# Chunked attention on one core: each half of a group's inverse T finished for itself, the second in the group's own first slot

## The chip, the cores and the metric

The kernel runs on one core of a Trainium2 chip. The core's engines are named as the profile names them: PE (matmuls) with its weight loads PEld, DVE (vector work), ACT (activations and copies), POOL (more vector work), SP (issues most DMAs). PSUM is the memory that PE writes into, SBUF the one that all engines share. The time is device microseconds of one execution, and the median of several executions is what is compared.

## What is computed

Three stages follow each other: a recurrent attention over 4 batches, 8 heads, 768 steps and 40 dimensions per head; a mixture of 8 experts of which each token takes one; and a second two-layer network.

```python
for t in range(S):                       # attention, state is D x D for each batch and head
    y[:, :, t] = r_t @ state
    Sa = state @ a_t
    state = state * w_t - outer(Sa, b_t) + outer(v_t, k_t)
...
expert_idx = argmax(x @ w_gate)          # experts: one of 8 for each token
out[mask] = gate_w * (relu(x[mask] @ w1[e]) @ w2[e])
...
h = x @ w_in                             # second network
return (max(h, 0) + alpha * min(h, 0)) @ w_out
```

## The kernel before

**Groups and slots.** The recurrence is cut into chunks of 64 steps. Four chunks (256 steps) of two batches form a group, so there are six groups: three one after the other for each pair of batches. A group is worked off in eight slots, one for each chunk and batch, 48 slots in all. A slot n runs `stage_a` (`sa`, L650) of its own, then `stage_v`, `stage_p` (`pp`, L610, with its copy `pw`, L612) and `stage_r` (`rp`, L638) of slot n + 1, then its `stage_c` (`yc`, L666) and later `stage_d`. All six groups' slots are one chain through the state `sm`.

**What a group needs before its first slot.** `prepare` makes scans of the decay on DVE (`s`, L455, and `q`, L457) and multiplies on POOL (`kb`, L460, and `abd`, L464; on DVE for `kb` in the start group). `products` multiplies them on PE for each of four sets `pg` and two chunks: `lp` (L483), whose parts ACT copies to `l1` and `l2` (L484, L485) and DVE masks into `la` (L491); `sides` adds two transpositions on PE, `bp` (L503) and `ap` (L507). Each of these three takes a bank of the PSUM ring `w1`, which has two.

**The inverse T.** From `l1` and `l2` the generator `inverse` makes the triangular inverse T of the group, the tile `tt`, in two halves of two chunks each. It transposes `l2` to `ul` (L522), does 31 steps of a multiplication `tmp` (L539) and a subtraction `ut` (L541) on DVE, has ACT check the result and `l1` (L424, a sum of squares, written to `ul` as waste), transposes `ut` twice on DVE (`ttc`, L547, and `t11`, L548), and copies the diagonal blocks of both halves into `tt` (L553, four instructions for each half, on POOL; on DVE for half 0 of the start group). Then, for each half, `zp` on PE (L567), its copy `z` by ACT (L570), `yp` on PE (L575) and its negated copy into `tt` by ACT (L577). `stage_p` of the first four slots reads half 0, that of the last four half 1. The banks for `zp` and `yp` are from `w1` in the start group, where eight matmuls with ones fill each of them first (`fill`, L238), and from the ring `mg` elsewhere, which has one bank, and from which the 31 steps of every group after the first take their `tmp` as well.

**What sets the order.** The generator stops at each `yield`, and a table places its pieces: with `n0` the first slot of the group before, the first 16 pieces are placed in slot `n0`, the next 4 in slot `n0 + 2`, the rest in slot `n0 + 8`, which is the group's own first. That is the order of the text only. A scheduler then walks over a modelled time line and takes on each engine what it holds ready, earlier text first, so an instruction may stand far from where the text puts it; only the very start, ahead of the first products, has its order written by hand. After the attention the experts and the second network follow; they start when the attention's tokens are there.

Of the kernel before, what the change touches and what calls it, by code (L numbers as in the profile page):

```python
# [19 lines left out]
P = 128  # L20
# [211 lines left out]
def whole(gen):  # L232
    for _ in gen:
        pass
# [49 lines left out]
class Attention:  # L284
# [230 lines left out]
    def inverse(self, o):  # L515

        nc = self.nc
        l1, l2 = o.l1, o.l2
        o.tt = [self.ringed("tt", self.tt) for _ in range(2)]
        ut = self.ut0 if o.start else self.unit()  # L520
        ul = self.pa.tile([P, 32, 32], F32, name="ul", tag="t4", bufs=3)
        nc.vector.transpose(ul, l2.rearrange("p c u j -> p j (c u)"))  # L522
        yield
        for j in range(31):
# [16 lines left out]
            nc.vector.tensor_tensor(ut[:, j + 1:, :m], ut[:, j + 1:, :m], tv, op=ALU.subtract)  # L541
            if j % 2:
                yield
        self.check(ut, ul, 0.01)
        self.check(l1.rearrange("p c u j -> p (c u) j"), ul, 0.01)
        t11, ttc = self.t4("t11"), self.t4("ttc")
        nc.vector.transpose(ttc.rearrange("p c u t -> p t (c u)"), ut)  # L547
        nc.vector.transpose(t11.rearrange("p c u s -> p s (c u)"), ut.rearrange("p t s -> p s t"))  # L548
        for half in range(2):
            for q in (1, 3, 0, 2):  # L550
                r = slice(32 * q, 32 * q + 32)
                eng = nc.vector if o.start and half == 0 else nc.gpsimd
                eng.tensor_scalar(o.tt[half][r, :, :, 32 * q:32 * q + 32], ttc[r, 2 * half:2 * half + 2], 1.0, 0.0, op0=ALU.mult, op1=ALU.add)  # L553
        yield

        lows = [slice(q * 64, q * 64 + 32) for q in range(2)]
# [1 line left out]
        both = [(c2, u, q) for c2 in range(2) for u in range(8) for q in range(2)]  # L558
        for half in range(2):
            if half:  # L560
                yield
            tt = o.tt[half]
            zp = self.work("zp", [P, 2, 8, 32], "w1" if o.start else "mg")
            if o.start:
                self.fill(zp, 8)
            for c2, u, q in both:
                nc.tensor.matmul(zp[lows[q], c2, u], lhsT=l1[highs[q], 2 * half + c2, u, :], rhs=tt[highs[q], c2, u, highs[q]], start=True, stop=True)  # L567
            z = self.pa.tile([P, 2, 8, 32], F32, name="z1", tag="z1", bufs=1)
            for lo in lows:
                nc.scalar.copy(z[lo], zp[lo])  # L570
            yp = self.work("yp", [P, 2, 8, 32], "w1" if o.start else "mg")
            if o.start:
                self.fill(yp, 8)
            for c2, u, q in both:
                nc.tensor.matmul(yp[lows[q], c2, u], lhsT=t11[lows[q], 2 * half + c2, u, :], rhs=z[lows[q], c2, u, :], start=True, stop=True)  # L575
            for lo, hi in zip(lows, highs):
                nc.scalar.activation(tt[lo, :, :, hi], yp[lo], AF.Copy, scale=-1.0)  # L577
            yield
# [119 lines left out]
    def run(self, rt, sp, moe, ctx):  # L698
        tc, nc = self.tc, self.nc
        os = []  # L700
        for bp in range(B // 2):
            for g in range(S // SL):
                o = K()
# [6 lines left out]
        def at(slot, place, fn):  # L710
            plan.setdefault((slot, place), []).append(fn)
# [19 lines left out]
        def start_inverse(o, n0):  # L731
            inv = self.inverse(o)
            at(n0, 0, lambda: [next(inv) for _ in range(16)])
            at(n0 + 2, 1, lambda: [next(inv) for _ in range(4)])
            at(n0 + 8, 0, lambda: whole(inv))

        def first(o):
# [8 lines left out]
        o = os[0]  # L746
# [10 lines left out]
        inv = self.inverse(o)  # L757
# [7 lines left out]
            whole(self.rest())  # L765
        for _ in range(17):
            next(inv)
        self.slots_room()
        at(1, 1, lambda: whole(inv))
        with tc.issue_after(o.last_v.ins), tc.issue_after(o.last_s.ins), tc.issue_after(o.last_g.ins):  # L770
            first(os[1])
        at(2, 0, self.empty)
        start_inverse(os[1], 0)
        for i in range(2, len(os)):
            lay(os[i], per * (i - 1))
# [558 lines left out]
```

## Time and profile before

| | us |
|---|---|
| median of 3 executions | 1142.77 |
| lowest and highest | 1138.71 and 1146.21 |
| the profiled execution | 1138.26 |
| span of its instructions | 1136.5 |
| its slots of group 0, 1, 2, 3, 4, 5 begin at | 86.2, 171.4, 257.6, 327.2, 402.6, 459.1 |
| attention ends at about | 510 |
| last step L541 of the inverse for group 1, 2, 3, 4, 5 ends at | 155.2, 236.6, 298.4, 381.0, 442.2 |

All starts are counted from the start of the span. The time of an execution lies 1.8 us above the span of its instructions. A group is called after its place, 0 to 5, and group 0 is also the start group, since its preparation has no slots to run beside. A boundary is the time between the last step of a group's inverse and the first `sa` of that group.

### The profile page before, as it was taken

How to read it: one execution, taken by the hardware profiler on the slowest of the kernel's cores; microseconds unless marked ns; L12 is line 12 of the kernel's file. 1: busy time of each engine (PE TensorE's matmuls, PEld its weight loads, DVE VectorE, ACT ScalarE, POOL GpSimd, SP SyncE). 2: the span in 40 equal slices, each digit the busy share in tenths (PEclk: the TensorE clock that was granted, in tenths of full speed). 3: DMA queues.
4: the chain of work that ended last, by engine and by line, in shares of the span. 5: the costliest groups of instructions: out<-in, count | busy, mean ns of one | idle time of the engine just before them, and what ended most of it. 6: DMA issues, size and time to landing. Idle time of an engine off the chain costs nothing.

```text
span 1136.5 us, 24811 instructions
## 1 busy us (share of the span) xinstructions
PE 1005.8 (88%) x9597; PEld 888.8 (78%) x9597; DVE 700.4 (62%) x1469; ACT 571.9 (50%) x1441; POOL 546.4 (48%) x496
## 2 busy tenths in 40 slices
PE   2639898879899898798888889999999999999997
PEld 2538777767687687678787769999999999999996
DVE  9865878978859678444699983324444444453542
ACT  3647687767788778774554444432222222121211
POOL 6717476672865624133664445452535343434332
PEclk8659899978899999799899999999999999999999
DMA  4623232322332124325787776430000000000000
GB/s 119 188 68 98 65 81 79 93 74 65 78 101 80 43 46 109 95 66 180 212 276 242 253 234 172 122 110 21 25 24 24 24 25 24 24 24 23 25 1 26
DMA packets 98080, 103.35 MB, mean 91 GB/s; under 512 B 58404, under 2 KB 78884, under 8 KB 97956
## 3 DMA queue, kind: packets, MB, share of 16 engines
q1 hardware_dynamic: 95652, 93.83, 28.8%
q0 software_dynamic: 2304, 7.87, 2.2%
q8 instruction: 78, 1.28, 0.5%
q14 instruction: 46, 0.38, 0.1%
HBM read 79.39 MB, written 22.28 MB: 89 GB/s over the span
## 4 chain that ended last, share of the span: by engine, by line
PE 56%; DVE 19%; ACT 9%; issue 5%; DMA 5%; POOL 4%; SPq 1%; DVEq 0%; ACTq 0%; POOLq 0%
PE ph L238 20%; PE po L238 19%; PE sa L650 2%; PE pp L610 2%; PE lp L483 2%; DMA raw<-in_moe_w_dram 2%; DVE ut L541 2%; DVE tmp L539 2%; PE yc L666 2%; DVE s L455 2%; DVE dec L215 2%; DVE q L457 2%; PE rp L638 1%; DVE dec L216 1%; POOL tt L553 1%
## 5 line engine op out<-in xcount | busy, mean ns | idle before, releaser
L229 POOL TENSOR_TENSOR gl<-g,gh 128x512 fp32r<-128x512 f32 x96 | 123.9, 1294 | 211.1 <-ACT gh L228 132.9
L228 ACT ACTIVATE gh<-g 128x512 fp32r<-128x512 f32 x96 | 60.7, 632 | 249.4 <-DVE g L1224 178.1
L1223 DVE TENSOR_SCALAR g<-ph,al 128x512 f32<-128x512 f32 x96 | 72.1, 751 | 156.9 <-POOL gl L229 79.1
L238 PE MATMUL ph<-x2thi,win 128*128 128x512 f32 x480 | 157.0, 392 | 0.0
L238 PE MATMUL po<-wout,gh 128*128 128x320 f32 x768 | 139.1, 309 | 0.0
L238 PEld LDWEIGHTS po<-wout,gh 128*128 128x128 f32 x768 | 122.0, 188 | 5.4
L238 PE MATMUL ph<-x2tlo,win 128*128 128x512 f32 x288 | 113.5, 394 | 0.0
L238 PE MATMUL po<-we,hh 128*128 128x320 f32 (+1 forms) x480 | 91.8, 317 | 18.5 <-DVE hh L1099 13.7
L238 PE MATMUL ph<-xthi,we 128*128 128x448 f32 (+2 forms) x360 | 96.6, 340 | 3.0 <-DVE hl L1099 2.9
L238 PEld LDWEIGHTS ph<-x2thi,win 128*128 128x128 f32 x480 | 88.5, 188 | 13.2
L238 PEld LDWEIGHTS po<-we,hh 128*128 128x128 f32 (+1 forms) x480 | 74.3, 183 | 24.9 <-DVE hh L1099 16.3
L238 PE MATMUL po<-wout,gl 128*128 128x320 f32 x384 | 82.9, 311 | 0.0
L624 POOL TENSOR_SCALAR_AFFINE_SELECT va<-vg 64x512 f32<-64x512 f32 x48 | 35.3, 734 | 88.3 <-ACT vg L623 59.5
L238 PE MATMUL ph<-xtlo,we 128*128 128x448 f32 (+2 forms) x216 | 73.4, 341 | 0.3 <-DVE xtlo L271 0.3
L464 POOL TENSOR_TENSOR abd<-ra,q 40x512 f32<-40x512 f32 x44 | 62.0, 1409 | 22.2 <-DVE q L457 7.2
L483 PE MATMUL lp<-kb,abd 128*128 128x128 f32 x352 | 56.0, 304 | 17.1 <-DMA tt<-in_kbP_dram 11.0
L238 PEld LDWEIGHTS ph<-xthi,we 128*128 128x128 f32 x360 | 65.5, 192 | 6.9 <-issue 2.5
L1224 DVE SCALAR_TENSOR_TENSOR g<-ph,g 128x512 f32<-128x512 f32 x96 | 66.3, 691 | 3.1
L238 PEld LDWEIGHTS po<-wout,gl 128*128 128x128 f32 x384 | 64.1, 188 | 2.8
L541 DVE TENSOR_TENSOR ut<-ut,tmp 128x31 f32<-128x31 f32 (+15 forms) x186 | 62.7, 337 | 4.1
L610 PE MATMUL pp<-tt,la 128*104 128x128 f32 x384 | 61.2, 307 | 3.9 <-DVE lg L912 2.2
L483 PEld LDWEIGHTS lp<-kb,abd 128*128 128x128 f32 x352 | 47.9, 209 | 19.8 <-POOL abd L464 13.3
(214 smaller groups left out, 2330.2 us busy)
## 6 DMA issues: line engine op xcount, KB each, us to landing
raw<-in_moe_w_dram SPq DMA_DIRECT2D x16, 512.0 KB
rv<-in_rvP_dram SPq DMA_DIRECT2D x48, 160.0 KB
raw<-in_moe_w_dram SPq DMA_DIRECT2D x16, 480.0 KB
kb<-in_kbP_dram SPq DMA_DIRECT2D x44, 160.0 KB
r<-in_moe_w_in_dram SPq DMA_DIRECT2D x10, 512.0 KB
r<-in_moe_w_out_dram SPq DMA_DIRECT2D x10, 512.0 KB
xs_d<-tt SPq DMA_DIRECT2D x8, 560.0 KB
raw<-in_moe_w_dram SPq DMA_DIRECT2D x16, 256.0 KB
```

Source lines behind the costliest of these rows:

```text
L215: nc.vector.scalar_tensor_tensor(t, up, 0xC0000000, t, op0=ALU.bitwise_and, op1=ALU.bitwise_or)
L228: nc.scalar.activation(hi, src, AF.Copy)
L229: return lo_eng.tensor_tensor(lo, src, f32(hi), op=ALU.subtract)
L238: return nc.tensor.matmul(out, lhsT=lhsT, rhs=rhs, start=start, stop=stop)
L455: nc.vector.tensor_tensor_scan(s[:, ::-1], wz[:, 1:][:, ::-1], self.d1s[:, ::-1], 0.0, ALU.mult, ALU.max)
L464: nc.gpsimd.tensor_tensor(abd[r, :, q * C:(q + 1) * C], ra[r], qc[r, :, :C], op=ALU.mult)
L483: nc.tensor.matmul(lp[:, i], lhsT=abd[:, i, c2, :], rhs=kb[:, i, c2, :], start=True, stop=True)
L541: nc.vector.tensor_tensor(ut[:, j + 1:, :m], ut[:, j + 1:, :m], tv, op=ALU.subtract)
L610: nc.tensor.matmul(pp[:, i], lhsT=o.la[x.half][:, x.c2, u, :], rhs=o.tt[x.half][:, x.c2, u, :], start=True, stop=True)
L624: nc.gpsimd.affine_select(x.va[:C].rearrange("p a b c -> p (a b) c")[:, :, D:], x.vg[:C].rearrange("p a b c -> p (a b) c")[:, :, D:], patt ...
L1223: nc.vector.tensor_scalar(g, ph, 0.0, al[:, f:f + 1], op0=ALU.min, op1=ALU.mult)
L1224: nc.vector.scalar_tensor_tensor(g, ph, 0.0, g, op0=ALU.max, op1=ALU.add)
```

## The change

The half of T that the first four slots read is finished alone, and the other half is left for the group's own first slot: the table places two pieces instead of four in slot `n0 + 2`, and diagonal, checks, `zp` and `yp` of half 1 come from slot `n0 + 8`. In the start group half 1 is placed in slot 0 instead of 1. Each of the two transpositions of `ut` becomes two of half the size, `ttc` first, with the diagonal of half 0 between `ttc` and `t11`. The checks come behind them, the first in place on `ut`, the second written to `ttc` as waste, so behind the diagonal of half 1, which reads `ttc`. And `zp` and `yp` take their banks from `mg` for half 0 and for the whole start group, from `w1` for half 1 of the other groups.

```diff
--- before.py
+++ after.py
@@ -541,16 +541,20 @@
             nc.vector.tensor_tensor(ut[:, j + 1:, :m], ut[:, j + 1:, :m], tv, op=ALU.subtract)
             if j % 2:
                 yield
-        self.check(ut, ul, 0.01)
-        self.check(l1.rearrange("p c u j -> p (c u) j"), ul, 0.01)
-        t11, ttc = self.t4("t11"), self.t4("ttc")
-        nc.vector.transpose(ttc.rearrange("p c u t -> p t (c u)"), ut)
-        nc.vector.transpose(t11.rearrange("p c u s -> p s (c u)"), ut.rearrange("p t s -> p s t"))
-        for half in range(2):
+
+        def diagonal(half):
             for q in (1, 3, 0, 2):
                 r = slice(32 * q, 32 * q + 32)
                 eng = nc.vector if o.start and half == 0 else nc.gpsimd
                 eng.tensor_scalar(o.tt[half][r, :, :, 32 * q:32 * q + 32], ttc[r, 2 * half:2 * half + 2], 1.0, 0.0, op0=ALU.mult, op1=ALU.add)
+
+        ttc = self.t4("ttc")
+        for t in range(0, 32, 16):
+            nc.vector.transpose(ttc.rearrange("p c u t -> p t (c u)")[:, t:t + 16], ut[:, t:t + 16])
+        diagonal(0)
+        t11 = self.t4("t11")
+        for t in range(0, 32, 16):
+            nc.vector.transpose(t11.rearrange("p c u s -> p s (c u)")[:, t:t + 16], ut.rearrange("p t s -> p s t")[:, t:t + 16])
         yield
 
         lows = [slice(q * 64, q * 64 + 32) for q in range(2)]
@@ -558,9 +562,12 @@
         both = [(c2, u, q) for c2 in range(2) for u in range(8) for q in range(2)]
         for half in range(2):
             if half:
+                diagonal(1)
+                self.check(ut, ut, 0.01)
+                self.check(l1.rearrange("p c u j -> p (c u) j"), ttc.rearrange("p c u t -> p (c u) t"), 0.01)
                 yield
             tt = o.tt[half]
-            zp = self.work("zp", [P, 2, 8, 32], "w1" if o.start else "mg")
+            zp = self.work("zp", [P, 2, 8, 32], "mg" if o.start or half == 0 else "w1")
             if o.start:
                 self.fill(zp, 8)
             for c2, u, q in both:
@@ -568,7 +575,7 @@
             z = self.pa.tile([P, 2, 8, 32], F32, name="z1", tag="z1", bufs=1)
             for lo in lows:
                 nc.scalar.copy(z[lo], zp[lo])
-            yp = self.work("yp", [P, 2, 8, 32], "w1" if o.start else "mg")
+            yp = self.work("yp", [P, 2, 8, 32], "mg" if o.start or half == 0 else "w1")
             if o.start:
                 self.fill(yp, 8)
             for c2, u, q in both:
@@ -731,7 +738,7 @@
         def start_inverse(o, n0):
             inv = self.inverse(o)
             at(n0, 0, lambda: [next(inv) for _ in range(16)])
-            at(n0 + 2, 1, lambda: [next(inv) for _ in range(4)])
+            at(n0 + 2, 1, lambda: [next(inv) for _ in range(2)])
             at(n0 + 8, 0, lambda: whole(inv))
 
         def first(o):
@@ -765,8 +772,9 @@
             whole(self.rest())
         for _ in range(17):
             next(inv)
+        next(inv)
         self.slots_room()
-        at(1, 1, lambda: whole(inv))
+        at(0, 0, lambda: whole(inv))
         with tc.issue_after(o.last_v.ins), tc.issue_after(o.last_s.ins), tc.issue_after(o.last_g.ins):
             first(os[1])
         at(2, 0, self.empty)
```

What stood on a line of `inverse` stands lower now: diagonal L549, `ttc` L553, `t11` L557, `zp` L574, `z` L577, `yp` L582, its copy L584, `pp` L617, `pw` L619, `sa` L657.

The scheduler's order on PE around `zp` of the start group, before. The number behind a name is the buffer's; `lp_673` is the first product of group 1, and the sixteen fills of `zp` and `yp` stand ahead of this piece.

```order
L567 MATMUL zp_544<-tt0_124,l1_180 32x32 x32
L575 MATMUL yp_588<-z1_585,t11_532 32x32 x32
L483 MATMUL lp_673<-kb0_107,abd0_109 128x128 x4
L503 MATMUL bp_681<-ident_60,kb0_107 128x104 x4
L610 MATMUL pp_904<-tt0_124,la_182 104x128 x4
L621 MATMUL rvp_910<-rv0_399 64x64 x8
L507 MATMUL ap_687<-ident_60,abd0_109 128x104 x4
```

The same place after the change; `lp_755` and `lp_796` are the fourth and the fifth of group 1's eight products.

```order
L483 MATMUL lp_755<-kb1_108,abd1_110 128x128 x4
L503 MATMUL bp_765<-ident_60,kb1_108 128x104 x4
L507 MATMUL ap_771<-ident_60,abd1_110 128x104 x4
L483 MATMUL lp_796<-kb0_107,abd0_109 128x128 x4
L503 MATMUL bp_804<-ident_60,kb0_107 128x104 x4
L507 MATMUL ap_810<-ident_60,abd0_109 128x104 x4
L483 MATMUL lp_817<-kb0_107,abd0_109 128x128 x4
L503 MATMUL bp_825<-ident_60,kb0_107 128x104 x4
L574 MATMUL zp_540<-tt0_124,l1_180 32x32 x32
```

Six of the eight products of group 1, with six `bp` and five `ap`, stand ahead of the start group's `zp` now; before, all of them stood behind its `yp`.

The order on DVE at the end of the start group's steps, before.

```order
L539 TENSOR_TENSOR tmp_524<-ul_292,ut_210 128x60
L541 TENSOR_TENSOR ut_210<-ut_210,tmp_524 128x2x30
L539 TENSOR_TENSOR tmp_527<-ul_292,ut_210 128x31
L541 TENSOR_TENSOR ut_210<-ut_210,tmp_527 128x31
L547 STREAM_TRANSPOSE ttc_533<-ut_210 128x32x32
L548 STREAM_TRANSPOSE t11_532<-ut_210 128x32x32
L553 TENSOR_SCALAR tt0_124<-ttc_533 32x16x32 x4
```

And after it; `la_673` and `la_794` are masks of group 1's products, `s_1531` and `q_1524` scans for group 2.

```order
L541 TENSOR_TENSOR ut_210<-ut_210,tmp_524 128x2x30
L455 SCALAR_TENSOR_TENSOR s_1531<-wz0_105,d1s0_116 104x520
L539 TENSOR_TENSOR tmp_527<-ul_292,ut_210 128x31
L491 TENSOR_TENSOR la_673<-lp_755,negmask0_133 128x4x64
L456 RECIPROCAL d1q0_119<-s_1531 104x8
L541 TENSOR_TENSOR ut_210<-ut_210,tmp_527 128x31
L457 SCALAR_TENSOR_TENSOR q_1524<-wz0_105,d1q0_119 104x520
L553 STREAM_TRANSPOSE ttc_530<-ut_210 128x16x32 x2
L557 STREAM_TRANSPOSE t11_537<-ut_210 128x16x32 x2
L491 TENSOR_TENSOR la_794<-lp_796,negmask0_133 128x4x64
L549 TENSOR_SCALAR tt0_124<-ttc_530 32x16x32 x4
```

Between the last but one step and the diagonal there are now two scans, a reciprocal and two masks, and `t11` ahead of the diagonal. Further up, masks of the same kind stand three times between the steps.

The order on PE at the boundary of groups 1 and 2, before; `tt1_125` is half 0 of T of group 2 and `tt2_126` half 1, `pp_3123` the first that reads half 0.

```order
L567 MATMUL zp_2393<-tt1_125,l1_1634 32x32 x32
L507 MATMUL ap_3198<-ident_60,abd1_110 128x104 x4
L575 MATMUL yp_2429<-z1_2426,t11_2381 32x32 x32
L567 MATMUL zp_2464<-tt2_126,l1_1634 32x32 x32
L610 MATMUL pp_3123<-tt1_125,la_1636 104x128 x4
L638 MATMUL rp_3131<-rv0_399,bds0_411 64x64
```

After the change, at the same boundary; `pp_3052` is the one that reads half 0 first, `sa_3134` the first slot of group 2.

```order
L582 MATMUL yp_2429<-z1_2426,t11_2390 32x32 x32
L673 MATMUL yc_3073<-va1_403,kbr_795 40x104
L503 MATMUL bp_3092<-ident_60,kb1_108 128x104 x4
L507 MATMUL ap_3098<-ident_60,abd1_110 128x104 x4
L617 MATMUL pp_3052<-tt1_125,la_1563 104x128 x4
L645 MATMUL rp_3060<-rv0_399,bds0_411 64x64
...
L657 MATMUL sa_3134<-vg1_406,pw0_416 64x104 x7
L628 MATMUL rvp_3300<-rv0_399 64x64
L617 MATMUL pp_3312<-tt1_125,la_1563 104x128 x2
L507 MATMUL ap_3127<-ident_60,abd1_110 128x104 x4
L617 MATMUL pp_3312<-tt1_125,la_1563 104x128 x2
L574 MATMUL zp_3160<-tt2_126,l1_1561 32x32 x32
```

`zp` of half 1, which stood between `yp` of half 0 and `pp`, now stands behind the group's first `sa`.

## Rows read from the trace of the kernel before

**Rows 1.** The page: busy us, share and instructions by engine; the chain's share by engine.

```profile
PE 1005.8 (88%) x9597; PEld 888.8 (78%) x9597; DVE 700.4 (62%) x1469; ACT 571.9 (50%) x1441; POOL 546.4 (48%) x496
...
PE 56%; DVE 19%; ACT 9%; issue 5%; DMA 5%; POOL 4%; SPq 1%; DVEq 0%; ACTq 0%; POOLq 0%
```

**Rows 2.** Windows of the slots of groups 0 to 2: length, busy by engine, PEclk.

```profile
86.20:171.40 85.20, 77.98 (x1213) 65.55 (x1212) 61.45 (x148) 63.85 (x201) 53.01 (x56) 0.94 0.32 83
171.40:257.60 86.20, 71.20 (x1053) 60.62 (x1051) 71.50 (x166) 63.44 (x201) 59.81 (x64) 0.90 0.30 80
257.60:327.20 69.60, 62.57 (x997) 53.80 (x997) 49.04 (x142) 55.48 (x167) 37.74 (x47) 0.90 0.30 75
```

**Rows 3.** Windows, last step of an inverse to the next group's sa, five boundaries.

```profile
155.20:171.40 16.20, 14.49 (x380) 12.43 (x376) 9.83 (x23) 14.17 (x40) 13.73 (x18) 1.00 0.41 110
236.60:257.60 21.00, 13.10 (x321) 11.41 (x316) 14.25 (x15) 12.28 (x33) 19.23 (x23) 0.75 0.21 57
298.40:327.20 28.80, 23.32 (x506) 20.23 (x504) 13.81 (x31) 23.17 (x65) 21.97 (x30) 0.88 0.29 74
381.00:402.60 21.60, 18.76 (x390) 16.42 (x385) 9.04 (x22) 16.16 (x45) 11.17 (x18) 0.84 0.17 44
442.20:459.10 16.90, 13.00 (x339) 11.23 (x335) 8.08 (x19) 12.01 (x29) 9.01 (x14) 0.79 0.53 150
```

**Rows 4.** Timeline, start group's T: start, us, engine, instruction, [idle before <-releaser].

```profile
57.86 1.01 PE L238 MATMUL yp<-ones 128*128 128x128 bf16 x8 [1.00 <-ACT la L510]
...
70.22 1.93 DVE L547 STREAM_TRANSPOSE ttc<-ut 128x1024 f32<-128x1024 f32 x1 [1.24 <-ACT ul L424]
...
74.13 1.08 PE L638 MATMUL rp<-rv,bds 64*64 64x64 f32 x16 [15.26 <-DVE t L548]
...
80.53 2.08 PE L483 MATMUL lp<-kb,abd 128*128 128x128 f32 x8
...
83.11 0.42 DVE L491 TENSOR_TENSOR la<-lp,negmask 128x256 f32<-128x256 f32 x1 [6.77 <-ACT l L485]
...
86.15 0.39 PE L650 MATMUL sa<-vg,pw 128*64 128x104 f32 x2
```

**Rows 5.** Timeline, slot 3, from its sa to that of slot 4.

```profile
111.22 0.25 PE L650 MATMUL sa<-vg,pw 128*64 128x104 f32 x1
...
121.27 0.20 DVE L539 TENSOR_TENSOR tmp<-tmp,ut 128x31 f32<-128x31 f32 x1 [0.67 <-ACT tmp L536]
...
124.71 2.04 PE L610 MATMUL pp<-tt,la 128*104 128x128 f32 x8 [1.54 <-ACT tt L577]
...
129.30 0.61 PE L650 MATMUL sa<-vg,pw 128*64 128x104 f32 x2
```

**Rows 6.** Timeline, boundary of groups 1 and 2: T and its way to the first slot.

```profile
236.67 2.00 DVE L547 STREAM_TRANSPOSE ttc<-ut 128x1024 f32<-128x1024 f32 x1
...
240.24 5.40 POOL L553 TENSOR_SCALAR tt<-ttc 32x512 f32<-32x512 f32 x8
...
249.27 1.92 PE L567 MATMUL zp<-tt,l 32*32 32x32 f32 x64 [3.30 <-ACT tt L577]
...
251.12 2.04 PE L610 MATMUL pp<-tt,la 128*104 128x128 f32 x8
...
256.57 0.58 ACT L612 COPY pw<-pp 104x512 f32<-104x512 f32 x1
...
259.90 0.20 DVE L539 TENSOR_TENSOR tmp<-tmp,ut 128x31 f32<-128x31 f32 x1 [3.59 <-ACT tmp L536]
```

**Rows 7.** Costliest groups by line and form, the products' matmuls: us busy, mean ns of one.

```profile
L483 PE MATMUL lp<-kb,abd 128*128 128x128 f32 x352 | 56.0, 304 | 17.1 <-DMA tt<-in_kbP_dram 11.0 <-DVE la L491 4.0 <-POOL abd L464 2.0
```

**Rows 8.** One line's instructions (L455 on DVE): ns min/median/max, first and last start.

```profile
L455 DVE TENSOR_TENSOR_SCAN s<-wz,d1s x24: 1202/1430/2206, 4.9 to 345.4; 104x520 f32<-104x520 f32 x24
```

**Rows 9.** One line's instructions (L553 on POOL), same columns.

```profile
L553 POOL TENSOR_SCALAR tt<-ttc x44: 607/611/1491, 72.5 to 449.6; 32x512 f32<-32x512 f32 x44
```

## Prediction, made before the changed kernel ran

> **What bounds the kernel now.** First the page: PE is busy for 88% of the span, its weight loads for 78%, no other engine for more than 62%, and the chain that ended last is PE's for 56%, DVE's for 19% and ACT's for 9% [rows 1]. That is a mean over an attention of about 425 us and 625 us of large matmuls behind it, so the windows come next. In group 0's slots PE is busy for 78.0 of 85.2 us, in group 1's for 71.2 of 86.2 and DVE for 71.5, in group 2's PE for 62.6 of 69.6 [rows 2]. What is the bound changes along a group. While an inverse runs, DVE is nearly full: outside its closing boundary group 1 has 86.2 - 21.0 = 65.2 us with 71.50 - 14.25 = 57.3 us of DVE, 88% [rows 2, 3]. In the boundary the group's end waits for one chain, T's way to the first slot, and the engines have gaps: the five boundaries take 104.5 us, DVE is busy for 55.0 of it, and in four of them PEclk falls to between 0.75 and 0.88 [rows 3].
>
> The start has a gap of its own. From 58.9 to 74.1 PE does nothing (15.26 us of idle) and then `rp`, `zp` and `yp` of the start group's T; the first product of group 1 comes at 80.53, behind them [rows 4]. The reason is a ring: the ones filled into `zp` and `yp` hold both banks of `w1` from about 57 on ([rows 4] has the second fill), and every product needs one. So group 1's products run in the slots of group 0, and its inverse takes its first step at 121.27, in slot 3 [rows 5]. That slot also waits for half 1 of the start group's T: `pp` comes at 124.71, after an ACT copy into T, and the slot takes 129.30 - 111.22 = 18.1 us, where a slot of group 0 takes 85.2/8 = 10.7 in the mean [rows 2, 5].
>
> **The change part by part: the start.** `zp` and `yp` leave `w1` for `mg`, so the products can run in PE's gap. The order on PE puts six `lp`, six `bp` and five `ap` ahead of `zp`, and DVE follows: their masks come between the steps, and two scans for group 2 ahead of the diagonal. New on DVE before T: four masks of 0.42 us before the last step and one after it [rows 4], two scans of 1.43 us (the middle one of their line) [rows 8] and a reciprocal, taken like the smallest step at 0.20 [rows 5]: 2.1 + 2.9 + 0.2 = 5.2. The eight fills of `yp` now wait for `mg`'s only bank, so their 1.0 us [rows 4] lies between `z` and `yp`. The two cuts cost 0.3 (next part). The wait of `ttc` for ACT's check, 1.24 us [rows 4], is gone. Sum: 5.2 + 1.0 + 0.3 - 1.2 = 5.3; the first `sa` comes 5.3 us later. The mask that stands ahead of the diagonal waits for its product, behind it are diagonal, `zp` and all of T; nothing shows when `kb` and `abd` are ready for it. Below, the masks can fill small gaps of DVE and leave +2; above, one product that is late by its own length and its evictions, about 5 us, gives +10.
>
> **Group 0's slots.** 17 pieces of four matmuls leave them. With 56.0 us for 352 `lp`, 0.159 us each [rows 7] (a bound from above for `bp` and `ap`, which have fewer columns), that is 17 x 4 x 0.159 = 10.8 us. PE is busy for 0.915 of these slots [rows 2]; at that share they get 10.8/0.915 = 11.8 us shorter. Slot 3 lies 7.4 us above the mean slot; since products run in it too and are counted already, I take 3 of that for the end of the wait for half 1, which is now made around slot 0. Together -15. Below: nothing but the wait, -3; above: all of it, -19.
>
> The Trainium skill (Perfetto Trace Analysis, Identifying the Most-Contended Engine) says that busy matmuls are no good measure of how near PE is to its limit and that the share of weight loads is. Here they stand for 65.55 of 85.20 us, 77% [rows 2], and by that measure the moved products would shorten nothing; the chain's 56% on PE speaks for mine. It is the third rival below.
>
> **The boundaries.** Before: after the last step `ttc` whole (2.00), POOL's eight copies in one row (5.40), `zp`, `z`, `yp`, the copy into T, then half 1's `zp` in PE's queue ahead of `pp`, and ACT's second `z` ahead of `pw` [rows 6]. After, only the second part of `ttc` is behind the last step (1.0); four copies on POOL at 0.61 (2.4) [rows 9]; `zp` and `yp` at 1.92 each, as they took at the low clock; two ACT copies at 1.16; `pp` 2.04 and `pw` 0.58 [rows 6]. That is 1.0 + 2.4 + 3.8 + 2.3 + 2.0 + 0.6 = 12.1, and with 2.4 us for queues as in the shortest boundary now, 14.5. Against 16.2, 21.0, 28.8 and 21.6 [rows 3] this is 29.6 us less; the fifth boundary I leave out, for there 28 of half 1's 32 `zp` still stand ahead of `yp` of half 0. But what runs beside the chain has to run in any case: in these four boundaries PE is busy for 69.7 of 87.6 us [rows 3], so at the same clock no more than 17.9 can go. I take 11, some six tenths, since the next inverse also begins earlier: its `tmp` waited 3.59 us [rows 6] with the bank of `mg` held by half 1, which has `w1` now. Ends: 0, if what is saved waits for DVE later, and -27, if the clock comes back as well (69.7 us of PE at a mean of about 0.87 would take 9 us less).
>
> `t11` is hidden beside POOL's 2.4 us of copies as long as it follows `ttc` at once. The checks have two new waits. ACT's check of `ut` comes after `t11`, about 2.0 + 1.2 us behind `ttc`, while `z` behind it in ACT's queue waits for `zp` until 2.4 + 1.9: no cost. The check of `l1` waits for the diagonal of half 1, and T's copy of half 0 is behind it: the second rival. `zp` and `yp` of half 1 take banks of `w1`, which products wait for; with few products early in a group I set that at nothing, and up to 3 us at each boundary are within the zero end. No DMA is added.
>
> Of the cuts: a step of 31 numbers takes 0.20 us, a mask of 256 takes 0.42 [rows 4, 5], so some 0.17 us of an instruction don't depend on its size. Two more for each of six inverses are 12 x 0.17 = 2 us of DVE, which only the start pays (0.3); elsewhere the first part of `ttc` goes between the steps. The Trainium skill (VectorE: DVE Perf Modes, on the TRN2 errata) speaks against cutting: an operation from SBUF pays a fixed latency each time, and few large tiles are better. By that rule alone the sum would be 2 us worse; that part of T is ready a microsecond earlier at each boundary is worth more where T is waited for.
>
> **Sum.** 5.3 - 15 - 11 = -20.7 us. Against the profiled execution, 1138.3, this is 1117.6; the median lies 4.5 above it, and I predict from the median, 1142.8 - 20.7 = 1122. What follows the attention is set by its end, so the shift passes through whole.
>
> **Rivals.** (1) DVE is the bound and the gain goes there. For it: 88% between the boundaries. Then the boundaries give 0, group 0 half of its 15, the start its 5.3: +5.3 - 7.5 = -2.2, 1141. Against it: 49.5 us of DVE's idle time in the boundaries. (2) Slower: ACT's check of `l1`. If POOL's copies take the slowest price of their row, 1.49 us [rows 9], half 1's diagonal ends 6.0 us after half 0's, the check at 7.2, while the copy into T could go after 1.9 + 1.2 + 1.9 = 5.0: 2.2 us at each of five boundaries, and every `pp` behind it. It decides from a diagonal of over 3.8 us on (5.0 - 1.2). For it: POOL is busy for 19.2 of 21.0 us there [rows 3]. With the start at its upper end and half of group 0's gain: 10 - 7.5 + 11 = +13.5, 1156. Against it: the two diagonals stand next to each other on POOL, or with one instruction between. (3) PE is not what limits group 0: only slot 3's wait goes there, 5.3 - 3 - 11 = -8.7, 1134. (4) The boundaries give all they can, with the clock: 5.3 - 15 - 27 = -36.7, 1106. That the halves aren't separated at all would be a case of (1): it is so at the fifth boundary.
>
> **Chances.** Forecast 0.46, its own range 1112 to 1131; (1) 0.14; (2) 0.10; (3) 0.10; (4) 0.20. About 1%, 11 us, is what a measurement of this kernel can tell from no change. Faster: 0.46 + 0.20 = 0.66; the same: 0.14 + 0.10 = 0.24; slower 0.10. The range leaves out (2) and the tails: 1102 to 1146.
>
> **What would show it.** Right: products of group 1 in PE's gap from 59 to 74, the first `sa` near 91, the first step of group 1's inverse before slot 2, slot 3 near 10 us, boundaries of 14 to 17 us with `pp` ahead of half 1's `zp`, PEclk near 1.0 there. Wrong: DVE without gaps between boundaries and slots that grow by what boundaries lose; ACT idle before the copy into T with POOL's diagonal as its releaser; products idle before half 1's `zp`.

## The result, and the profile after

| | before | after |
|---|---|---|
| median, us | 1143.03 | 1128.53 |
| profiled execution, us | 1138.26 | 1124.41 |
| its span | 1136.5 | 1122.7 |
| its groups' first slots begin at | 86.2, 171.4, 257.6, 327.2, 402.6, 459.1 | 93.6, 161.0, 236.0, 309.8, 377.2, 442.1 |

The ratio is 0.987 (95% interval 0.984 to 0.990): 14.5 us faster, where 20.7 were forecast and 1102 to 1146 was the range. The two profiled executions differ by 13.9 us, and their rows tell where from. Three later executions stand apart from the others of their kernel, one of the changed kernel at 2319 us and two of the kernel with half 1 in `mg` at 1146 and 1149 us, and they are named below where a number includes them.

The page of the changed kernel, its first part, reads like that of before [rows 1]: no engine has much less to do, so the time comes from idle time.

```profile
PE 1010.3 (90%) x9597; PEld 891.3 (79%) x9597; DVE 691.9 (62%) x1481; ACT 570.2 (51%) x1441; POOL 551.6 (49%) x496
```

The windows of its six groups' slots (the last one up to the last slot's `sa`), columns as in [rows 2]:

```profile
93.60:161.00 67.40, 61.80 (x1008) 52.49 (x1002) 52.02 (x139) 55.04 (x171) 39.15 (x44) 0.97 0.30 78
161.00:236.00 75.00, 66.77 (x1015) 55.97 (x1014) 56.87 (x157) 58.39 (x183) 49.17 (x53) 0.93 0.30 81
236.00:309.80 73.80, 65.23 (x1001) 54.39 (x1001) 57.58 (x152) 57.37 (x178) 45.59 (x53) 0.93 0.33 82
309.80:377.20 67.40, 61.52 (x1028) 52.68 (x1023) 57.36 (x155) 56.58 (x176) 43.01 (x50) 1.00 0.30 76
377.20:442.10 64.90, 57.18 (x1009) 47.31 (x1008) 41.82 (x138) 49.47 (x143) 20.81 (x30) 0.89 0.22 53
442.10:492.30 50.20, 44.87 (x621) 37.16 (x619) 23.64 (x70) 38.64 (x108) 13.14 (x17) 0.86 0.37 100
```

and for the kernel before, group 5 up to the same point:

```profile
459.10:505.10 46.00, 39.86 (x564) 33.13 (x560) 23.82 (x70) 38.48 (x107) 12.35 (x17) 0.89 0.30 75
```

The first slot begins 7.4 us later (93.6 against 86.2). Group 0 takes 67.4 instead of 85.2 us, 17.8 less [rows 2]. Groups 1 to 5 take 75.0, 73.8, 67.4, 64.9 and 50.2 against 86.2, 69.6, 75.4, 56.5 and 46.0 ([rows 2] for the first two; the others are differences of the table's starts): -11.2, +4.2, -8.0, +8.4 and +4.2, in all -2.4. What follows the attention is 1.0 shorter. 7.4 - 17.8 - 2.4 - 1.0 = -13.8. So 10.4 of it is there when group 1's first slot begins (161.0 against 171.4).

The five boundaries after the change, in the order of [rows 3]:

```profile
148.00:161.00 13.00, 11.55 (x239) 9.78 (x239) 6.57 (x15) 11.79 (x33) 10.69 (x15) 1.00 0.29 75
218.90:236.00 17.10, 16.11 (x290) 13.47 (x288) 7.85 (x23) 14.29 (x41) 12.76 (x18) 0.96 0.26 75
290.80:309.80 19.00, 16.70 (x294) 14.15 (x295) 7.96 (x22) 15.08 (x43) 12.78 (x20) 0.79 0.26 66
361.80:377.20 15.40, 14.02 (x285) 12.03 (x279) 9.47 (x24) 14.55 (x43) 10.82 (x17) 1.00 0.24 63
424.10:442.10 18.00, 11.86 (x280) 10.31 (x276) 4.81 (x11) 9.66 (x23) 8.21 (x12) 0.62 0.15 40
```

They take 82.5 us, 22.0 less than before, and four of the five are shorter, as forecast. Groups 1 to 5 keep 2.4 of it. The rest is given back outside the boundaries. One stretch shows that best: from the first step of group 1's inverse to the last step of group 5's, in the kernel before and then in the changed one.

```profile
121.50:442.20 320.70, 285.09 (x4398) 242.15 (x4391) 253.43 (x689) 248.87 (x765) 178.13 (x204) 0.93 0.28 72
```

```profile
102.60:424.10 321.50, 291.66 (x4545) 244.57 (x4546) 255.53 (x722) 260.42 (x807) 182.28 (x209) 0.96 0.30 76
```

320.7 and 321.5 us, though four of the boundaries lie in it and went from 87.6 to 64.5. The rest of the stretch grew from 233.1 to 257.0. DVE has 253.4 and 255.5 us of work in the stretch. Of this, 46.9 lay in the four boundaries before [rows 3] and 31.9 do now, so 15 us of it left them: the scans `s` and `q` (8.1 us), the first part of `ttc` (3.7) and the transposition to `ul` (2.1) are most of that. DVE is about as full outside the boundaries as it was: (253.4 - 46.9)/(320.7 - 87.6) = 89% before, (255.5 - 31.9)/(321.5 - 64.5) = 87% after. But PE is too: (285.1 - 69.7)/233.1 = 92% and (291.7 - 58.4)/257.0 = 91%. The shares alone don't say which of the two holds the slots. The stretch only begins 18.9 us earlier, at 102.6.

The start, timeline of the changed kernel, where [rows 4] show the same place:

```profile
73.08 0.18 DVE L541 TENSOR_TENSOR ut<-ut,tmp 128x31 f32<-128x31 f32 x1
...
82.91 1.16 ACT L577 COPY z<-zp 32x512 f32<-32x512 f32 x2 [2.57 <-PE zp L574]
...
84.73 2.07 PE L483 MATMUL lp<-kb,abd 128*128 128x128 f32 x8
...
87.38 1.20 PE L582 MATMUL yp<-z,t 32*32 32x32 f32 x64
...
93.63 0.94 PE L657 MATMUL sa<-vg,pw 128*64 128x104 f32 x16
...
102.37 0.20 DVE L539 TENSOR_TENSOR tmp<-tmp,ut 128x31 f32<-128x31 f32 x1
```

The products of group 1 run in PE's gap, as forecast, and the first step of its inverse comes before slot 2 (102.37; 121.27 in [rows 5]). The last step of the start's inverse ends at 73.26. Before, it ended at 68.98, so T is 4.3 us late by then, and 5.4 at the end of `z` (84.07, before 78.64). The largest single addition comes next: between the end of `z` and `yp` (87.38) lie 3.3 us, where the sum had 1.0. In them stand `lp` of group 1's last set, 2.07 us (at a granted clock of 0.56 between 84.7 and 87.4), and the fill. Some of this is made up again before the first `sa`. The same three places in the kernel before:

```profile
68.78 0.20 DVE L541 TENSOR_TENSOR ut<-ut,tmp 128x31 f32<-128x31 f32 x1
...
77.46 1.18 ACT L570 COPY z<-zp 32x512 f32<-32x512 f32 x2 [1.07 <-PE zp L567]
...
78.69 1.91 PE L575 MATMUL yp<-z,t 32*32 32x32 f32 x62 [0.29 <-ACT z L570]
```

Slot 3 takes 6.7 us (120.77 - 114.08) where it took 18.1 [rows 5]; its `pp` comes without a wait.

```profile
114.08 0.93 PE L657 MATMUL sa<-vg,pw 128*64 128x104 f32 x16
...
115.87 1.12 PE L617 MATMUL pp<-tt,la 128*104 128x128 f32 x8
...
120.77 0.76 PE L657 MATMUL sa<-vg,pw 128*64 128x104 f32 x12
```

The fifth boundary, timeline of the changed kernel:

```profile
428.57 2.67 POOL L549 TENSOR_SCALAR tt<-ttc 32x512 f32<-32x512 f32 x4 [1.81 <-DMA xs_d<-xr,sli]
...
433.40 1.54 PE L574 MATMUL zp<-tt,l 32*32 32x32 f32 x49 [0.39 <-POOL tt L549]
...
434.75 1.06 ACT L424 ACTIVATE ttc<-l 128x1024 f32<-128x1024 f32 x1 [1.71 <-POOL tt L549]
...
434.89 1.58 PE L582 MATMUL yp<-z,t 32*32 32x32 f32 x52
...
436.67 1.18 ACT L584 ACTIVATE tt<-yp 32x512 f32<-32x512 f32 x2 [0.78 <-PE zp L574]
```

POOL comes to the diagonal of half 0 late, behind a transfer of the expert router (`xs_d`), and `zp` of half 1 stands in PE's queue ahead of `yp` of half 0 and waits for POOL's second diagonal. `z` had been done since 433.04. ACT's check of `l1` waits there too, for 1.71 us, but T's copy at 436.67 was released by PE, not by the check.

### The profile page after: what moved, and what is told of

The parts are those of the page before. It is cut to its first block, busy times and chain, and to the rows that moved or that the text cites. A ratio compares the mean times of both kernels' runs of the same rounds, so it can differ in the third digit from the quotient of the medians.

```text
span 1122.7 us, 24830 instructions
## 1 busy us (share of the span) xinstructions
PE 1010.3 (90%) x9597; PEld 891.3 (79%) x9597; DVE 691.9 (62%) x1481; ACT 570.2 (51%) x1441; POOL 551.6 (49%) x496
## 5 line engine op out<-in xcount | busy, mean ns | idle before, releaser
L238 PE MATMUL po<-we,hh 128*128 128x320 f32 (+1 forms) x480 | 91.9, 318 | 17.8 <-DVE hh L1107 13.1
L464 POOL TENSOR_TENSOR abd<-ra,q 40x512 f32<-40x512 f32 x44 | 64.3, 1461 | 22.6 <-PE ap L507 11.6
L657 PE MATMUL sa<-vg,pw 128*64 128x104 f32 x768 | 58.2, 269 | 8.3 <-ACT vg L647 8.0
L617 PE MATMUL pp<-tt,la 128*104 128x128 f32 x384 | 60.9, 306 | 5.0 <-DVE lg L920 2.4
L694 POOL TENSOR_TENSOR yt<-rs,q 104x256 f32<-104x256 f32 x46 | 33.5, 729 | 64.4 <-DVE rs L693 25.2
```

What stands on the lines that cost most here:

```text
L238: return nc.tensor.matmul(out, lhsT=lhsT, rhs=rhs, start=start, stop=stop)
L464: nc.gpsimd.tensor_tensor(abd[r, :, q * C:(q + 1) * C], ra[r], qc[r, :, :C], op=ALU.mult)
L617: nc.tensor.matmul(pp[:, i], lhsT=o.la[x.half][:, x.c2, u, :], rhs=o.tt[x.half][:, x.c2, u, :], start=True, stop=True)
L657: nc.tensor.matmul(sa[q * 64:q * 64 + 64, i], lhsT=x.pw[:, i, q * C:(q + 1) * C], rhs=x.vg[:, i, q, :], start=True, stop=True)
L694: eng.tensor_tensor(yt[:PP, :, x.c2 * C:x.c2 * C + C], x.rs, x.o.q[x.half][:, x.p4, x.c2, :C], op=ALU.mult)
```

## Experiments

All ratios are against the kernel before on the same chip, with 95% intervals. The kernel before took 1150.8 us beside the first four kernels, 1143.5 beside the next four and 1149.4 beside the last four, so medians of different batches aren't compared without their ratios. The changed kernel ran only beside a kernel before of 1143 us, never beside one of 1149 to 1151. Where a kernel of the first four or the last four is compared with the changed one, the difference between chips is in the comparison.

**The start's part alone** (`e1_start_only`), on the kernel before:

```diff
-            zp = self.work("zp", [P, 2, 8, 32], "w1" if o.start else "mg")
+            zp = self.work("zp", [P, 2, 8, 32], "mg")
...
             next(inv)
+        next(inv)
         self.slots_room()
-        at(1, 1, lambda: whole(inv))
+        at(0, 0, lambda: whole(inv))
```

(`yp` likewise.) Expected: 

> The kernel before with only the start's part of the change: zp and yp of the start group take their banks from mg, and its half 1 is placed in slot 0; everything on the later groups is as before. Theory A (the gain is the start's: group 1's products run in PE's gap and slot 3 no longer waits for half 1, while what the boundaries gain is given back in the slots behind them): about 1131 us, 10 to 14 below the kernel before, group 0's slots some 17 us shorter, the first slot some 6 later. Rival B (the gain comes from the boundaries): the later first slot eats group 0's gain, 1139 to 1143.

Measured: 1135.35 us, ratio 0.988 (0.985 to 0.992). By the ratio this part alone gives about the whole gain, 13.7 us. In its profile group 1's first step comes at 109.9, 11.6 us earlier than in the profile before, slot 3 takes 6.1 us and group 0 72.8, 12.4 less. But its first slot comes at 101.0, 14.8 later, where 6 were expected; that is 4.6 later than in the kernel with whole transpositions on the same chip (96.4), which has the later checks too. Against the one profile of the kernel before, taken on another chip, its span is only 3.4 us shorter (1133.1), so the profiles don't show all of the 13.7.

**The rest alone** (`e2_rest_only`), on the changed kernel:

```diff
-            zp = self.work("zp", [P, 2, 8, 32], "mg" if o.start or half == 0 else "w1")
+            zp = self.work("zp", [P, 2, 8, 32], "mg" if half == 0 and not o.start else "w1")
...
-        next(inv)
         self.slots_room()
-        at(0, 0, lambda: whole(inv))
+        at(1, 1, lambda: whole(inv))
```

(`yp` likewise.) Expected: 

> The change without the start's part: zp and yp of the start group in w1 and its half 1 in slot 1 as before; the parted transpositions, the later checks, half 1 in the group's own first slot and its banks stay. Theory A: 1137 to 1143, no difference from the kernel before that is clear, with boundaries some 20 us shorter in all and the time between them longer by as much. Rival B: 1128 to 1132, as the whole change.

Measured: 1139.76 us, ratio 0.989 (0.986 to 0.993). That is in theory A's range in us and against it by the ratio: the rest gives a gain of its own, about 12 us. With the start's 14 this would make 26, and the whole change had 14.5 and, later, 13. Whether the two parts don't add up stays open: the whole change didn't run in this batch, and the kernel with whole transpositions, which differs from it in the cut alone, has 0.978 here, as the two parts together would (0.988 x 0.989 = 0.977). The profiled execution was the slowest of its six (1144.22) and doesn't show where the gain lies: boundaries of 93.5 us in all (sum row), 11 less than before, and the stretch of inverses again at 320.7.

```profile
sum 93.50, PE 82.91 PEld 70.73 DVE 43.24 ACT 72.00 POOL 69.42; mean PE 16.58 PEld 14.15 DVE 8.65 ACT 14.40 POOL 13.88
```

**Half 1 in `mg`** (`e4_half1_in_mg`), on the changed kernel:

```diff
-            zp = self.work("zp", [P, 2, 8, 32], "mg" if o.start or half == 0 else "w1")
+            zp = self.work("zp", [P, 2, 8, 32], "mg")
```

(`yp` likewise.) Expected: 

> The change with zp and yp of half 1 in mg, as before, in every group. If the ring mg held back the next inverse's first step, as the kernel before suggests, that step comes 3 to 5 us later after each boundary and the time is 5 to 15 us above the changed kernel, 1134 to 1143. If products that need w1 are what half 1 disturbs, the time falls below the changed kernel, 1120 to 1127.

Measured: 1137.9 us, ratio 0.989 (0.984 to 0.994) over all six executions; the four from 1129 to 1139 us have a median of 1133.8, 0.985 of the kernel before. No difference from the changed kernel's 0.987 is clear, in either direction, and the interval leaves room for some 5 us. So nothing here shows that the bank of half 1 matters, on which the prediction counted for the next inverse.

**Whole transpositions** (`e3_whole_transposes`, and again on another chip as `e8_whole_again`):

```diff
-        for t in range(0, 32, 16):
+        for t in range(0, 32, 32):
-            nc.vector.transpose(ttc.rearrange("p c u t -> p t (c u)")[:, t:t + 16], ut[:, t:t + 16])
+            nc.vector.transpose(ttc.rearrange("p c u t -> p t (c u)")[:, t:t + 32], ut[:, t:t + 32])
```

(`t11` likewise.) Expected: 

> The change with ttc and t11 as one transposition each. If the cut matters at the boundaries, each of five gets 1 us longer: 1131 to 1136, 3 to 7 above the changed kernel. If what a boundary saves is given back behind it: within 2 us of the changed kernel, 1127 to 1131, or less by the 0.17 us of each instruction that goes.

> The changed kernel with whole transpositions, once more on another chip, where it was 0.978 of the kernel before against 0.987 and 0.989 of the changed one. If cutting the transpositions costs time (twelve more instructions on DVE, and t11's second part ahead of the slot's own work): 0.976 to 0.981 again. If that was the chip: 0.985 to 0.989.

Measured: 1127.27 us, ratio 0.978 (0.974 to 0.981), and 1125.89, 0.979 (0.976 to 0.982). No run shows that the cut brings anything: without it the kernel is the fastest here, by either measure, of those that make all of T. What the cut costs stays open, since the two never ran in one batch: 3 us by the medians, 10 by the ratios. In both batches here the kernel before took longer than beside the changed one. The five boundaries did get longer without the cut, 89.3 and 89.1 us against 82.5 and 86.6 in the changed kernel's two profiles, and the time did not.

Profiles of one chip now say where the gain lies. Group 1's first slot begins at 173.8 with the start's part alone, at 180.3 with the rest alone, and at 163.0 with whole transpositions, which have both. From there to the last slot's `sa`, in the same order:

```profile
173.80:501.10 327.30, 293.09 (x4536) 246.76 (x4532) 239.31 (x664) 258.61 (x776) 165.92 (x195) 0.92 0.30 78
```

```profile
180.30:509.70 329.40, 299.00 (x4596) 250.84 (x4596) 235.12 (x667) 259.98 (x776) 164.49 (x197) 0.92 0.30 76
```

```profile
163.00:495.40 332.40, 300.47 (x4663) 252.64 (x4661) 238.87 (x664) 262.49 (x784) 168.25 (x202) 0.92 0.31 78
```

Their boundaries take 95.8, 93.5 and 89.3 us, and the groups behind get no shorter with them. What both parts have over each alone was there before group 1 began.

**The changed kernel again** (`after_again`), the base of the next three.

> The changed kernel once more, unchanged, beside the next three on one chip. Both theories expect 0.985 to 0.989 of the kernel before on this chip.

Measured: 1131.3 us (1130.9 without the execution of 2319 us), ratio 0.989 (0.985 to 0.992).

**Products twice on PE** (`e5_products_twice`) **and 21 us more of DVE** (`e6_steps_twice`), both on the changed kernel:

```diff
+        for _ in range(2 if (o.bp, o.g) > (0, 1) else 1):
             for i in range(4):
                 nc.tensor.matmul(lp[:, i], lhsT=abd[:, i, c2, :], rhs=kb[:, i, c2, :], start=True, stop=True)
...
+            for _ in range(2 if (o.bp, o.g) > (0, 1) and j % 2 == 0 else 1):
                 nc.vector.tensor_tensor(tv, col.unsqueeze(2).to_broadcast([P, n, m]),
                                         ut[:, j, :m].unsqueeze(1).to_broadcast([P, n, m]), op=ALU.mult)
```

(The first loop is `e5`, the second `e6`.) Expected: 

> The changed kernel with the four lp matmuls of each product done twice for groups 2 to 5 (same operands, same result): 32 times four matmuls, at 0.159 us each 20 us more of PE and nothing more on another engine. Theory A (PE is full at 0.9 of every slot, so the boundaries' 22 us could not be kept): +18 to +24 us over the changed kernel. Rival B (DVE's inverse is what the slots wait for): +0 to +7.

> The changed kernel with every other multiplication tmp of the inverses of groups 2 to 5 done twice (same operands, same result): 4 x 16 instructions of some 0.34 us, 21 us more of DVE, all of it in the row of steps. Theory A (PE is the bound): +0 to +8 us over the changed kernel. Rival B (DVE's inverse is the bound): +16 to +22.

Measured: 1134.42 us (ratio 0.993, 0.990 to 0.996) and 1145.05 (1.001, 0.998 to 1.003), which is +3.1 and +13.8 over the changed kernel on that chip; the second is short of rival B's range and above theory A's. The stretch of inverses, for the changed kernel, with the products twice, and with the steps twice:

```profile
104.90:433.40 328.50, 301.05 (x4544) 252.57 (x4544) 256.47 (x722) 260.43 (x808) 181.21 (x209) 0.92 0.29 74
```

```profile
105.80:432.80 327.00, 312.54 (x4802) 267.99 (x4803) 256.10 (x722) 261.96 (x807) 179.08 (x209) 0.99 0.29 75
```

```profile
103.70:442.50 338.80, 298.36 (x4404) 252.99 (x4402) 272.72 (x771) 254.46 (x785) 180.85 (x205) 0.88 0.27 71
```

The matmuls `lp` alone, in the first two of these:

```profile
104.90:433.40 328.50, 38.39 (x253) 32.50 (x251) 13.45 (x32) 13.87 (x64) 0.92 0.29 74
```

```profile
105.80:432.80 327.00, 69.98 (x509) 61.55 (x508) 13.41 (x32) 14.00 (x64) 0.99 0.29 75
```

The expectation counted four instructions for a product where the trace has eight (x8 in [rows 4]), so the products took not 20 but 31.6 us more in this stretch. All other matmuls, as many as before, took 20.1 us less, at a granted clock of 0.99 instead of 0.92, so that PE has 11.5 us more in all, and the stretch is 1.5 shorter. Theory A as it was worded falls with this: PE went from 92% of the stretch to 96%, so 0.9 was not its limit. That PE holds the slots at a given clock is not excluded, since two thirds of what was added came back with the higher clock. With 16.3 us more of DVE the stretch is 10.3 longer, at a clock of 0.88. Here the Trainium skill (Perfetto Trace Analysis, Identifying the Most-Contended Engine) had the better sign: by the weight loads PE stood at 252.6/328.5 = 77%, just below DVE's 256.5/328.5 = 78%, and it was DVE's extra work that cost.

**A shorter start** (`e7_start_mended`), on the changed kernel:

```diff
-            zp = self.work("zp", [P, 2, 8, 32], "mg" if o.start or half == 0 else "w1")
+            zp = self.work("zp", [P, 2, 8, 32], "mg" if half == 0 else "w1")
-            if o.start:
+            if o.start and half == 0:
                 self.fill(zp, 8)
...
-            if o.start:
-                self.fill(yp, 8)
...
+            with tc.issue_after(os[0].yp0.ins):
                 for c2 in range(2):
                     self.products(o, 3, c2)
...
+                with tc.issue_after(os[0].dg0.ins):
+                    self.prepare(o, 0)
```

(`yp` takes its banks as `zp` does. `yp0` is the last `yp` of half 0 of the start group, `dg0` its last diagonal on DVE; the last piece is for group 2.) Expected: 

> The changed kernel with a shorter start: half 1 of the start group takes its banks from w1 as the later groups' does, the fills of its zp and of both yp go, the products of group 1's last set come behind yp of half 0, and group 2's first scans behind the diagonal. What the trace of the changed kernel shows of them in the way of T is 3.0 us of scans on DVE, 2.1 us of a product and 0.9 us of a fill between z and yp: the first slot should come 4 to 6 us earlier, and the first step of group 1's inverse some 5 us, since mg is free. Theory A: 4 to 7 us below the changed kernel. Rival B, under which the inverse's start sets group 0's length: 8 to 12 below.

Measured: 1135.86 us, ratio 0.994 (0.991 to 0.997), 4.6 us above the changed kernel, where both theories had it below. T of half 0 was ready at 87.7 and `pp` began at 88.35, against 92.13 in the changed kernel's profile of that batch, but the first `sa` came at 96.6 against 95.9. The timeline has the wait that took its place:

```profile
88.35 1.91 PE L618 MATMUL pp<-tt,la 128*104 128x128 f32 x8
...
88.98 2.31 POOL L460 TENSOR_TENSOR kb<-kb,s 104x512 f32<-104x512 f32 x2 [3.81 <-DMA kb<-in_kbP_dram]
...
91.32 2.20 DVE L455 TENSOR_TENSOR_SCAN s<-wz,d1s 104x520 f32<-104x520 f32 x1 [3.45 <-POOL kb L460]
...
93.56 0.20 ACT L461 COPY s<-s 104x8 f32<-104x8 f32 x1 [4.53 <-DVE s L455]
...
93.67 0.58 ACT L620 COPY pw<-pp 104x512 f32<-104x512 f32 x1
...
96.63 0.61 PE L658 MATMUL sa<-vg,pw 128*64 128x104 f32 x2
```

POOL waits for `kb`, DVE's scan for POOL, ACT's small copy `s` for the scan, and `pw` of slot 0 stands behind that copy.

**13 us more of DVE outside the steps** (`e9_masks_twice`) **and 20 us less in them** (`e11_fewer_steps`), on the changed kernel:

```diff
+        for _ in range(2 if (o.bp, o.g) > (0, 1) else 1):
             o.last_v = nc.vector.tensor_tensor(la[:, c2, p4, :C], lp[:, :, :C], self.negmask.unsqueeze(1).to_broadcast([P, 4, C]), op=ALU.mult)
...
+            if (o.bp, o.g) <= (0, 1) or j % 2 == 0:
                 nc.vector.tensor_tensor(ut[:, j + 1:, :m], ut[:, j + 1:, :m], tv, op=ALU.subtract)
```

(The first is `e9`, the second `e11`.) Expected: 

> The changed kernel with the mask la of every product of groups 2 to 5 made twice: 32 instructions of 0.42 us, 13.4 us more of DVE that stand outside the row of steps. If DVE's time as a whole is the bound while an inverse runs, as 21.6 us more in the row cost 14 us, it costs 7 to 11 us over the changed kernel (1.130 ms to 1.142 ms where that takes 1131). If only the row of steps counts: 0 to 3. If PE's slots are the bound: 0 to 3.

> The changed kernel without the subtractions at odd j in the inverses of groups 2 to 5 (15 of 31 in each, so T of these groups is not the inverse): 60 instructions of 0.34 us, 20 us less of DVE in the row of steps. If DVE's inverse is the bound: 10 to 15 us below the changed kernel, 0.975 to 0.979 of the kernel before. If PE is: 0 to 4 below.

Measured: 1145.52 us, ratio 0.997 (0.995 to 1.000), and 1124.03, 0.979 (0.975 to 0.982). Against the mean of the changed kernel's two ratios, 0.988, that is some +11 and -10 us, as the theory of DVE's time has it. But the changed kernel didn't run in this batch; whole transpositions did, and `e11` is no faster than they are (0.979 both). The profiles don't agree with the theory either. In that of `e9` groups 1 to 5 take 333.0 us (172.9 to 505.9), as they do in the changed kernel's second profile (167.2 to 500.2); what it has more lies in group 0 (76.4 against 71.4) and behind the attention. The stretch of inverses of `e11`:

```profile
102.90:424.60 321.70, 293.96 (x4407) 247.81 (x4407) 234.63 (x645) 253.92 (x785) 181.81 (x205) 0.92 0.29 74
```

21 us less of DVE than in the changed kernel's first profile, and the stretch is as long (321.7 and 321.5); in the second profile it was 328.5, so a difference of up to 7 us says little here. That DVE's time is paid for in the groups themselves is shown by `e6` alone, and upwards only; that less of it would save time is not shown.

**The addition on PE** (`e10_sum_on_PE`), on whole transpositions:

```diff
-                nc.tensor.matmul(x.yc[r, i, a:], lhsT=kb[:, c], rhs=x.va[:, i, q, a:], start=True, stop=True)
+                nc.tensor.matmul(x.yc[r, i, a:], lhsT=kb[:, c], rhs=x.va[:, i, q, a:], start=True, stop=False)
+            for b, d in ((slice(0, HQ), slice(0, HQ)), (slice(HQ, P), slice(HQ, PP))):
+                nc.tensor.matmul(x.yc[d, i, D:], lhsT=self.bds[b, u, :d.stop - d.start], rhs=x.r[b, u], start=False, stop=True)
...
-        nc.vector.tensor_tensor(x.rs, x.yc[:, :, D:], x.rs, op=ALU.add)
+        nc.scalar.copy(x.rs, x.yc[:, :, D:])
```

(The copy of `rp` into `rs` goes.) Expected: 

> With whole transpositions, and the addition of rp to yc (one DVE instruction of 0.41 us in each of 48 slots) replaced by 8 more matmul pairs on PE that accumulate in yc's bank, 0.68 us in each slot; ACT copies the sum in place of rp. DVE has 20 us less, PE 33 us more. If DVE's time is the bound: 6 to 13 us below the kernel with whole transpositions. If PE is: 15 to 30 above. A wait of yc's only bank for ACT in place of DVE would eat some of the gain.

Measured: 1178.64 us, ratio 1.025 (1.021 to 1.030), 53 us above the kernel with whole transpositions in the same batch. Its stretch of inverses, below that of whole transpositions:

```profile
106.00:428.40 322.40, 294.03 (x4496) 247.16 (x4494) 253.86 (x703) 258.77 (x799) 177.01 (x207) 0.94 0.29 75
```

```profile
106.10:457.50 351.40, 337.46 (x5032) 268.67 (x5028) 244.07 (x663) 257.28 (x790) 178.51 (x206) 0.97 0.26 68
```

DVE has 9.8 us less there, PE 43 more, and PE is busy for 96%. The 33 us of matmuls that were expected in the slots cost 53; whether PE's limit or the wait of `yc`'s one bank for ACT is more of it, this run doesn't tell.

## Why the prediction was right

**Direction and size.** Faster by over 1% was forecast and measured; of the 20.7 us, 14.5 came.

**The start, 5.3.** It was 7.4, within its ends. The terms up to the end of `z` were 5.2 + 0.3 - 1.2 = 4.3 and came to 5.4; the fill's 1.0 came to 3.3, since a product that isn't late stands with it in PE's queue; 1.3 of the two was made up before the first `sa`. The one attempt to take the price off by mending T's path (`e7_start_mended`) moved the wait to `kb`.

**Group 0's slots, -15.** They gave -17.8. The rows show what was forecast, products in the gap and slot 3 without its wait, and the start's part alone has 0.988 with the boundaries nearly as they were. How the 17.8 divide between the products, slot 3 (11.4) and the boundary at the group's end (3.2) isn't settled, for the inverse that starts 18.9 us earlier comes with all of them.

The 10.8 us of matmuls were right by luck. The sum took four instructions of 0.159 us for each piece, but an `lp` has eight (x8 in [rows 4]), so six `lp` and eleven others make 48 + 44 instructions and 14.6 us. On the other hand more of group 2's products came into the shorter slots: `lp`, `bp` and `ap` together, by windows of these tiles, take 29.5 us in group 0's slots before and 18.6 after, 10.9 less, for four products fewer and not six. That the slots shorten by this over PE's busy share is not shown either: `e5_products_twice` added 31.6 us of products to other groups and cost 3.1, at a higher clock.

**The boundaries, -11.** This is the step that was mis-sized: the sum turned what boundaries lose into time at six tenths, and 2.4 of 22.0 us were kept. They did shorten, by 22.0 us in the first profile and 17.9 in the second, but against the one profile before groups 1 to 5 kept 2.4 and 0.7 of it. The sum took PE's idle time as the bound of what can go and 0, "if what is saved waits for DVE later", as an end only. The stretch of inverses shows it at that end, 320.7 against 321.5, and so do the three kernels of one chip, whose groups 1 to 5 take 327 to 332 us with boundaries of 96 to 89. Rival (1), in its mechanism though not in its time, fits what the boundaries did: DVE is 87% busy between them, and `e6_steps_twice` shows that more of its time there costs. But PE is 91% busy there, and neither `e9_masks_twice` nor `e11_fewer_steps` shows DVE's price in the groups themselves, so which engine takes the saved time back is not shown. The size that rival (1) gave to group 0, half of 15, was wrong. Why each group came out as it did (+8.4 for group 4, -8.0 for group 3) isn't settled; the scheduler's order differs in all of them.

**The other rivals.** (2), ACT's check behind POOL's diagonal, decided nothing: its one long wait, 1.71 us in the fifth boundary, ended while PE was still at `yp`, and the next longest was 0.33. (3) kept only 3 us for group 0, which gave 17.8, so its sum was wrong; its view of PE isn't settled. (4) didn't happen: of the three boundaries among the first four that had a low clock [rows 3], two got it back (0.96, 0.79, 1.00; in the second profile 0.95, 0.77, 0.92, but there the first boundary has 0.69), and groups 1 to 4 kept 6.6 us in all.

**The cuts.** 0.17 us each was right, 0.16 here: two parts of `ttc` take 2 x 1.066 against 1.976 us.

```profile
L547 DVE STREAM_TRANSPOSE ttc<-ut x6: 1934/1976/2003, 70.2 to 442.7; 128x1024 f32<-128x1024 f32 x6
```

```profile
L553 DVE STREAM_TRANSPOSE ttc<-ut x12: 1008/1066/1085, 74.7 to 424.2; 128x512 f32<-128x512 f32 x12
```

That the microsecond saved at each boundary would be worth more isn't borne out: whole transpositions gave 0.978 and 0.979, though in other batches. That each instruction has a fixed price the Trainium skill (VectorE: DVE Perf Modes, on the TRN2 errata) and the trace agree; its advice of few large tiles fits these runs, and none of them shows a gain from the cut.

## What to carry to other kernels

A wait that is removed from a periodic kernel is a gain only if the work that it covered doesn't lengthen what runs between two such waits: take the stretch from one period's step to the same step some periods later, and ask which engine is full in it when the wait is gone. An engine's busy share doesn't say whether it is the limit. A few microseconds more of its work can say more, but look whether something else moved with them, as PE's granted clock did here. The gain that stayed was the one ahead of the first full period.

## What was not expected

DVE's four copies of the start group's diagonal took 2.43 us as one row before, with POOL's four beside them, and 3.69 in the changed kernel, where POOL first multiplied `kb` (2.50) beside them. Before and after:

```profile
73.90 2.43 DVE L553 TENSOR_SCALAR tt<-ttc 32x512 f32<-32x512 f32 x4
```

```profile
78.12 2.50 POOL L460 TENSOR_TENSOR kb<-kb,s 104x512 f32<-104x512 f32 x2
...
78.72 3.69 DVE L549 TENSOR_SCALAR tt<-ttc 32x512 f32<-32x512 f32 x4
```
